# Linear attention followed by a snake MLP on one core: a phased opening, and q transposed by a crossbar DMA from batch 3 on

## The chip, the cores and the metric

The kernel runs on one core of one Trainium2 chip. The metric is the time of one execution on the device in microseconds (us). Of the core's engines the text uses the short names of the profile: PE is TensorE (PEld is its weight load), DVE is VectorE, ACT is ScalarE, POOL is GpSimd, and SP is the engine whose queue issues nearly all DMAs.

## What is computed

The attention is linear: the softmax of q runs over the head's 64 columns, the softmax of k over the sequence, so that k and v collapse to one 64x64 matrix per head. Its output, reshaped to 4608 tokens of 512, goes through two matmuls with a "snake" between them.

```
q, k, v: [8 batches, 8 heads, 576, 64] f32;  w_in [512, 2048], w_out [2048, 512], alpha [2048]
q_s = softmax(q, axis=-1);  k_s = softmax(k, axis=2)
kv  = einsum('bhsd,bhse->bhde', k_s, v)
x   = einsum('bhsd,bhde->bhse', q_s, kv) -> [4608, 512]
h   = x @ w_in
g   = h + sin(alpha*h)**2 / alpha
out = g @ w_out                      # [4608, 512] f32
```

## The kernel before, in words

The schedule is written by hand: every engine runs its instructions in the order in which the program text issues them, and only semaphores and the number of buffers in a pool make one engine wait for another.

**Attention of one batch b.** `exp_q` and `exp_k` (two ACT instructions each, after a load of ACT's Exp table) turn the staged f32 inputs into bf16. `cast_v` copies v. `norm_q` sums q's exponentials on DVE, takes the reciprocal and multiplies (`engs` says on which engine): the result is `qn`, 128 partitions by 2304 bf16. `kv_mm` is 36 small matmuls into `kvp`. `kv_norm` divides on DVE. `q_transpose` makes `qT` out of `qn` by 18 TensorE transposes of 128x128 in two groups (12 and 6) through PSUM, and each group is copied out by `eng`. `attn_out`, called four times, does 4 matmuls each into `xp` and casts the result into `xT`, the transposed input of the MLP. The tiles `kvp`, `tp` (of the transposes) and `xp` share one PSUM slot, the pool `ps_a` with `bufs=1`, so each waits until the one before has been read out. (In the opening, batch 0 has a pool of its own with four.)

**MLP of one tile t of 512 tokens** (9 tiles). The first half, called h(t) here, has 16 slots `ni`. In each, `mm_h` does 4 matmuls of 512 columns into a PSUM tile `hp` (pool `ps_h`, 4 buffers), `sine` applies sin on ACT and squares it on ACT ("A"), POOL ("P") or DVE ("D"), and `combine` on DVE makes the bf16 tile `g`. The second half, o(t), is 64 matmuls `mm_o` for four output blocks j, each copied out by `evac_o` and stored by two DMAs of SP's queue. Exp and Sin need different ACT tables, so each change between them issues an ACT_TABLE_LOAD.

**Stages.** Batch 0's attention comes first, then h(0), o(0) with batch 1's attention at its end, and h(1) with batch 2's attention woven into its slots. From t = 2 on, a stage t holds h(t), o(t-1) and, up to t = 6, the attention of batch b = t+1: after slot 0 the exponentials, casts, `norm_q` on POOL and the loads of the next batch; at slot 4 `kv_mm` and `kv_norm`; at slots 6 and 7 the transposes; at slots 8 to 11 the four `attn_out`. After slot ni, o(t-1) has been advanced to `want` of its 64 matmuls:

```
want = 20 + 11 * ni // 4 if b is not None else 4 * (ni + 1)
```

Inputs and weights pass through a staging pool of 6 buffers (`stage`), so a load is issued only when the buffer six loads earlier has been consumed. All loads and stores stand in one SP queue in program order.

Of the kernel before, what the change touches and what calls it, by code (L numbers as in the profile page):

```python
# [15 lines left out]
F32 = mybir.dt.float32  # L16
BF16 = mybir.dt.bfloat16
# [6 lines left out]
def kernel(  # L24
# [74 lines left out]

    wst = {}  # L100

    def load_win(c):
        st = stage.tile([128, 4, 512], F32, name="st_w", tag="st")
        nc.sync.dma_start(out=st, in_=win_v[:, :, c * 512:(c + 1) * 512])
        wst["i", c] = st

    def load_wout(c):
# [64 lines left out]

# [130 lines left out]
    accs = [ps_o.tile([128, dm], F32, name="op", tag="o") for _ in range(2)]
    accs += [ps_h.tile([128, dm], F32, name="hp", tag="h") for _ in range(2)]
    for ni in range(nN):
        for j in range(4):
            mm_o(0, j, ni, accs[j])
# [3 lines left out]
    cast_v(1, [V, GP])
    for j in range(4):
        evac_o(0, j, accs[j], ACT_CP if j % 2 else DVE_CP)
    load_batch(2)
    for g in range(2):
        q_transpose(1, g, ps_a, ACT_CP)
    kv_mm(1, 0, ps_a)
    kv_mm(1, 1, ps_a)
    kv_norm(1)
    for ii in range(2):  # L320
        attn_out(1, ii, 0, ps_a, DVE_CP)
        attn_out(1, ii, 1, ps_a, ACT_CP)


    def o_stream(t):
        for j in range(4):
            acc = ps_o.tile([128, dm], F32, name="op", tag="o")
            for ni in range(nN):
                mm_o(t, j, ni, acc)
                if ni == nN - 1:  # L330
                    evac_o(t, j, acc, DVE_CP)
                yield

    SQ1 = "PAPDPAPDPAPDPAPA"
    for t in range(1, nT):
        b = t + 1 if t + 1 < B else None
        os = o_stream(t - 1) if t > 1 else None
        done = 0
        pend = None
        for ni in range(nN):  # L340
# [10 lines left out]
            s = sine(t, ni, hp, "A" if t > 1 else SQ1[ni])
            if t == 1:
                if pend:
                    combine(t, *pend)
                pend = (ni, hp, s)
            else:
                combine(t, ni, hp, s)
            if b is not None and ni == 0:
                exp_q(b)
                exp_k(b)  # L360
                cast_v(b, [GP, GP])
                norm_q(b, [GP])
                if b + 1 < B:
                    load_batch(b + 1)
            if os is not None:
                want = 20 + 11 * ni // 4 if b is not None else 4 * (ni + 1)
                while done < min(64, want):
                    next(os)
                    done += 1
        if pend:  # L370
            combine(t, *pend)
        if os is not None:
            for _ in os:
                pass

    for _ in o_stream(nT - 1):
        pass


# [28 lines left out]
```

## Time and profile before

| | before |
|---|---|
| time, median of 3 runs | 339.1 us (338.93 to 339.96) |
| the profiled execution: its time, and the span from first to last instruction | 340.48 us, 338.7 us |
| PE busy | 291.6 us (86%), 1713 matmuls |
| ACT busy | 237.5 us (70%) |
| DVE busy | 200.6 us (59%) |
| POOL busy | 71.7 us (21%) |
| DMA | 46.44 MB, 41.4% of 16 engines |

The span is what the profile divides up; 1.78 us of the profiled execution lie outside it. That execution is 1.4 us longer than the median. PE is the busiest engine, but its 14% of idle time are not spread evenly, and the busy share says nothing about the clock at which the matmuls ran, which the trace gives apart.

### The profile page before, as it was taken

The page shows a single profiled execution, that of the slowest core. Times are in us where ns is not written, and L with a number is a line of the kernel's source. Part 1 is how long each engine was busy: PE and PEld are TensorE (multiplying, and loading weights), DVE is VectorE, ACT ScalarE, POOL GpSimd, SP SyncE. Part 2 cuts the span into 40 slices and gives each one's busy share as a digit, 9 for nine tenths or more (in the row PEclk, how much of TensorE's full clock was granted, in tenths as well). Part 3 has the DMA queues.
Part 4 walks back from the last instruction along what each step waited for, and adds up shares of the span by engine and source line. Part 5 has one row for each costly group of instructions (what it writes and reads, how often), then busy time and mean ns, then how long its engine had stood idle before and what let it go on. Part 6 is the DMA issues. An engine that isn't in the chain of part 4 may idle for free.

```text
span 338.7 us, 4528 instructions
## 1 busy us (share of the span) xinstructions
PE 291.6 (86%) x1713; PEld 134.9 (40%) x1713; DVE 200.6 (59%) x286; ACT 237.5 (70%) x328; POOL 71.7 (21%) x47
## 2 busy tenths in 40 slices
PE   0585895484799899989998999899989999999994
PEld 0432342322334444443444445444534444444441
DVE  3648761206886786487558755874687545555511
ACT  4476862268479867986897789778968777777600
POOL 0456632026443700150024003300400000000000
PEclk9979999556999999999999999999999999999999
DMA  7999903999500111850195029302111111211132
GB/s 266 389 386 387 391 10 76 309 392 391 215 0 0 33 31 33 297 199 19 38 333 173 3 62 362 120 4 59 33 31 31 32 31 33 50 44 33 32 93 62
DMA packets 22758, 46.44 MB, mean 137 GB/s; under 512 B 1728, under 2 KB 1744, under 8 KB 22736
## 3 DMA queue, kind: packets, MB, share of 16 engines
q1 hardware_dynamic: 22736, 46.15, 41.4%
q8 instruction: 13, 0.21, 0.3%
q14 instruction: 9, 0.07, 0.1%
HBM read 36.71 MB, written 9.44 MB: 136 GB/s over the span
## 4 chain that ended last, share of the span: by engine, by line
PE 49%; ACT 21%; DVE 18%; issue 6%; POOL 2%; DMA 2%; SPq 0%; ACTq 0%; POOLq 0%
PE op L229 22%; PE hp L209 20%; ACT s L215 7%; DVE g L225 7%; ACT ke L117 3%; ACT qe L117 3%; ACT L215 2%; ACT L117 2%; ACT s L217 2%; PE xp L196 2%; DVE kvb L168 2%; PE hp L229 2%; DVE s L221 2%; DVE qT L184 2%; PE tp L183 2%
## 5 line engine op out<-in xcount | busy, mean ns | idle before, releaser
L209 PE MATMUL hp<-xT,win 128*128 128x512 bf16 x576 | 150.5, 389 | 12.4 <-DVE g L225 11.4
L225 DVE SCALAR_TENSOR_TENSOR g<-s,inva_sb,hp 128x512 bf16<-128x512 f32 x144 | 105.9, 744 | 70.4 <-ACT s L217 65.2
L229 PE MATMUL op<-wout,g 128*128 128x512 bf16 x544 | 138.6, 380 | 0.0
L215 ACT ACTIVATE s<-hp,alpha_sb 128x512 f32<-128x512 f32 x144 | 97.8, 683 | 49.7 <-PE hp L209 36.8
L209 PEld LDWEIGHTS <-win 128*128 128x128 bf16 x576 | 56.8, 100 | 84.5 <-issue 21.4
L217 ACT ACTIVATE s<-s 128x512 f32<-128x512 f32 x126 | 79.4, 630 | 4.0
L229 PEld LDWEIGHTS <-g 128*128 128x128 bf16 x576 | 53.8, 98 | 63.4 <-issue 0.5
L147 POOL TENSOR_TENSOR qn<-qe,qs 128x2304 bf16<-128x2304 bf16 (+1 forms) x7 | 26.7, 3817 | 115.2 <-PE hp L209 100.7
L145 DVE TENSOR_REDUCE qs<-qe 128x36 f32<-128x2304 bf16 (+1 forms) x10 | 20.7, 2071 | 27.2 <-ACT qe L117 27.2
L234 DVE COPY o<-op 128x512 f32<-128x512 f32 x33 | 22.3, 676 | 14.0 <-PE op L229 14.0
L183 PE MATMUL tp<-identb,qn 128*128 128x128 bf16 x144 | 11.9, 234 | 20.9 <-DVE qn L147 9.2
L199 DVE CAST xT<-xp 128x512 bf16<-128x512 f32 (+1 forms) x28 | 20.8, 745 | 5.5 <-PE xp L196 5.5
L219 POOL TENSOR_TENSOR s<-s 128x512 f32<-128x512 f32 x12 | 12.9, 1076 | 39.4 <-ACT s L215 39.4
L183 PEld LDWEIGHTS <-qn 128*128 128x128 bf16 x144 | 9.8, 104 | 26.7 <-issue 16.3
L117 ACT ACTIVATE qe<-st_q 128x1152 bf16<-128x1152 f32 x16 | 17.8, 1156 | 3.4 <-DMA st_q<-in_q_dram 3.4
L131 POOL CAST vb<-st_v 128x1152 bf16<-128x1152 f32 x14 | 16.9, 1236 | 15.2 <-DMA st_v<-in_v_dram 15.2
L117 ACT ACTIVATE ke<-st_k 128x1152 bf16<-128x1152 f32 x16 | 17.7, 1149 | 0.7 <-DMA st_k<-in_k_dram 0.7
L196 PE MATMUL xp<-qT,kvb 64*64 64x256 bf16 (+1 forms) x128 | 10.4, 320 | 5.4 <-DVE kvb L168 2.5
L156 PE MATMUL kvp<-vb,ke 64*128 64x130 bf16 x288 | 12.4, 252 | 0.9 <-ACT qT L184 0.9
L156 PEld LDWEIGHTS <-ke 64*128 64x128 bf16 x288 | 10.8, 112 | 4.2 <-ACT s L215 3.0
L215 ACT ACT_TABLE_LOAD x8 | 10.3, 1283 | 1.7 <-PE hp L209 1.6
L117 ACT ACT_TABLE_LOAD x8 | 10.3, 1283 | 0.9 <-PEq L392 0.7
(28 smaller groups left out, 75.8 us busy)
## 6 DMA issues: line engine op xcount, KB each, us to landing
out_dram<-o SPq DMA_DIRECT2D x72, 128.0 KB, 2.4
st_q<-in_q_dram SPq DMA_DIRECT2D x7, 1152.0 KB, 6.3
st_k<-in_k_dram SPq DMA_DIRECT2D x7, 1152.0 KB, 9.6
st_v<-in_v_dram SPq DMA_DIRECT2D x7, 1152.0 KB, 11.1
st_w<-in_moe_w_in_dram SPq DMA_DIRECT2D x4, 1024.0 KB, 13.6
st_w<-in_moe_w_out_dram SPq DMA_DIRECT2D x4, 1024.0 KB, 15.7
st_q<-in_q_dram SPq DMA_DIRECT2D x2, 576.0 KB, 4.3
st_k<-in_k_dram SPq DMA_DIRECT2D x2, 576.0 KB, 6.4
```

The lines of the kernel that those rows point to most:

```text
L117: nc.scalar.activation(dst[:, :, ii * 128:(ii + 1) * 128].rearrange("p j (x d) -> p x j d", x=2), src[:, ii::2], AX.Exp)
L145: nc.vector.tensor_reduce(part, src, axis=AXL.X, op=ALU.add)
L147: engs[h].tensor_tensor(dst, src, part.unsqueeze(3).to_broadcast([128, J, w, D]), op=ALU.mult)
L156: nc.tensor.matmul(kvp[:, e, ii * 130:(ii + 1) * 130], ke[r, j, ii * 128:(ii + 1) * 128], vt[r, j, ii * 130:(ii + 1) * 130], start=(j == 0 ...
L183: nc.tensor.transpose(tp[:, h, 2 * jj + ii], qn[:, j, ii * 128:(ii + 1) * 128], identb)
L199: eng(xT[:, ii::2, c0:c0 + n], xp[:, :, 0:n])
L209: nc.tensor.matmul(hp, win[:, ki, ni * 128:(ni + 1) * 128], xT[:, ki, t * MF:(t + 1) * MF], start=(ki == 0), stop=(ki == 3))
L215: nc.scalar.activation(s, hp, AX.Sin, scale=alpha_sb[:, ni:ni + 1])
L217: nc.scalar.activation(s, s, AX.Square)
L225: nc.vector.scalar_tensor_tensor(G[t][:, ni], in0=s, scalar=inva_sb[:, ni:ni + 1], in1=hp, op0=ALU.mult, op1=ALU.add)
L229: nc.tensor.matmul(acc, G[t][:, ni, j * 128:(j + 1) * 128], wout[:, ni, :], start=(ni == 0), stop=(ni == nN - 1))
L234: eng(o, acc)
```

## The change

The stages are taken apart and put in another order up to t = 2, and from batch 3 on `qn` is transposed by one DMA per batch through the DMA engines' crossbar.

- **Opening.** 14 matmuls on a tile that nobody reads (`warm`) stand on PE ahead of batch 0's transposes. The first half of `norm_q(0)` is multiplied on POOL, `cast_v(0)` is all on DVE, a one-element Sin issues the Sin table load ahead of the `xT` casts, and w_in's first chunk is loaded and cast in two parts. All of batches 1 and 2 are loaded ahead of the first stores.
- **h(0)** has 6 PSUM tiles (two of them of `ps_o`, `wide`) and 4 buffers for s, and squares in another rotation. **o(0)** is done in two pairs of blocks; batch 1's attention is woven into the second. **h(1)** stands alone. **o(1)** comes next with batch 2's attention woven in (50 of its 64 matmuls; the other 14 stand behind slot 2 of h(2)). **h(2)** carries batch 3's attention, and half its squares go to POOL.
- **Stages t = 3 to 6** keep their order, but `kv_mm` moves from slot 4 to 5, the transposes of slots 6 and 7 become one DMA_TRANSPOSE of SP's queue issued at slot 7, and the `attn_out` move from slots 8 to 11 to slots 10 to 13. h(7), h(8) and o(8) are as before; the last block is copied by DVE and ACT in halves and stored from two queues.
- `kv_norm` takes one reciprocal in place of two.

```diff
-    spool = ctx.enter_context(tc.tile_pool(name="spool", bufs=3))
+    spool = ctx.enter_context(tc.tile_pool(name="spool", bufs=4))
...
-        kvr = small.tile([128, 2, 2], F32, name="kvr")
+        kvr = small.tile([128, 2, 2, 2], F32, name="kvr")
...
-    def mm_h(t, ni):
+    def mm_h(t, ni, wide=False):
...
-        hp = ps_h.tile([128, MF], F32, name="hp", tag="h")
+        if wide and ni % 6 >= 4:
+            hp = ps_o.tile([128, MF], F32, name="op", tag="o")
+        else:
+            hp = ps_h.tile([128, MF], F32, name="hp", tag="h")
...
+        if last:
+            nc.vector.tensor_copy(o[:, 0:dm // 2], acc[:, 0:dm // 2])
+            nc.scalar.copy(o[:, dm // 2:], acc[:, dm // 2:])
...
+    load("q", q, 1)
+    load("k", k, 1)
+    load("v", v, 1, halves=True)
+    load_batch(2)
...
-        norm_q(0, [V, V])
-        cast_v(0, [GP, V])
...
+        warm = ps_s.tile([128, 4, 128], F32, name="warm", tag="a")
+        for n in range(14):
+            nc.tensor.matmul(warm, identb, A["qe", 0][:, 0:4, 0:128], start=True, stop=True)
+        norm_q(0, [GP, V])
+        cast_v(0, [V, V])
...
+        nc.scalar.activation(zero, zero, AX.Sin)
...
-    SQ0 = "APADAPADAPADAPAA"
...
+    SQ0 = "ADPADPADPADPADPA"
     for ni in range(nN):
...
+        h_slot(0, ni, SQ0[ni], lag, wide=True)
+        flush(lag, 1)
+        if ni in (0, 2, 5):
+            cast_win((0, 2, 5).index(ni) + 1, POOL_CP)
+        elif ni in (8, 11, 14):
+            cast_wout((8, 11, 14).index(ni), POOL_CP)
...
+    exp_q(1)
+    norm_q(1, [GP, V])
+    os = o_pair(0, 0, ps_o)
+    take(os)
+    exp_k(1)
+    cast_v(1, [GP, V])
+    os = o_pair(0, 2, ps_h)
+    take(os, 16)
+    q_transpose(1, 0, ps_a, ACT_CP)
+    take(os, 2)
+    q_transpose(1, 1, ps_a, ACT_CP)
...
+    SQ1 = "PAPDPAPAPPDPAPAP"
+    for ni in range(nN):
+        h_slot(1, ni, SQ1[ni], lag, wide=True)
+        flush(lag, 1)
...
+    attn_front(2, [V, GP])
+    os = o_stream(1)
+    take(os, 32)
+    kv_mm(2, 0, ps_a)
...
+    def attn_back(b, n):
+        if n == 0:
+            kv_mm(b, 0, ps_a)
+            kv_mm(b, 1, ps_a)
+            kv_norm(b)
+        elif n == 2:
+            A["qT", b] = att2.tile([128, J, 2, 128], BF16, name="qT")
+            nc.sync.dma_start(out=A["qT", b].rearrange("p j ii c -> p (j ii) c"),
+                              in_=A["qn", b].rearrange("p j c -> p (j c)"), transpose=True)
+        elif 5 <= n < 9:
+            attn_out(b, (n - 5) // 2, (n - 5) % 2, ps_a, DVE_CP)
+
+    SQ2 = "PAPAPAPAPAPAPAPA"
+    for ni in range(nN):
+        hp = h_slot(2, ni, SQ2[ni], lag)
+        flush(lag, 1)
+        if ni == 2:
+            flush(lag, 0)
+            attn_front(3, [GP])
+            take(os)
+        attn_back(3, ni - 7)
...
             if b is not None:
-                if ni == 4:
-                    kv_mm(b, 0, ps_a)
-                    kv_mm(b, 1, ps_a)
-                    kv_norm(b)
-                elif ni in (6, 7):
-                    q_transpose(b, ni - 6, ps_a, DVE_CP)
-                elif 8 <= ni < 12:
-                    attn_out(b, (ni - 8) // 2, ni % 2, ps_a, DVE_CP)
...
+                attn_back(b, ni - 5)
+            s = sine(t, ni, hp, "A")
+            combine(t, ni, hp, s)
```

How the change moves instructions is shown at three places. The first is SP's queue in one middle stage. Of the kernel before: the loads of the next batch, then the stores of o(t-1), two for each of the four blocks.

```order
L92 DMA st_q<-in_q_dram 128x4x576
L92 DMA st_k<-in_k_dram 128x4x576
L92 DMA st_v<-in_v_dram 128x4x576
L237 DMA out_dram<-o 64x512 x8
L92 DMA st_q<-in_q_dram 128x4x576
```

Of the changed kernel, the same stage:

```order
L92 DMA st_q<-in_q_dram 128x4x576
L92 DMA st_k<-in_k_dram 128x4x576
L92 DMA st_v<-in_v_dram 128x4x576
L248 DMA out_dram<-o 64x512 x4
L420 DMA_TRANSPOSE qT<-qn 128x18x128
L248 DMA out_dram<-o 64x512 x4
```

The transposing DMA stands behind the stores of blocks 0 and 1 and ahead of those of blocks 2 and 3.

The second place is DVE's queue in the same stage, from the copy of block 0 (`o<-op`) to the casts into `xT`. Of the kernel before:

```order
L234 COPY o<-op 128x512
L225 SCALAR_TENSOR_TENSOR g<-s,inva_sb,hp 128x512 x3
L167 RECIPROCAL kvr<-kvp 64x4
L168 TENSOR_TENSOR kvb<-kvp,kvr 64x256
L167 RECIPROCAL kvr<-kvp 64x4
L168 TENSOR_TENSOR kvb<-kvp,kvr 64x256
L225 SCALAR_TENSOR_TENSOR g<-s,inva_sb,hp 128x512 x2
L234 COPY o<-op 128x512
L184 COPY qT<-tp 128x1536
L225 SCALAR_TENSOR_TENSOR g<-s,inva_sb,hp 128x512
L184 COPY qT<-tp 128x768
```

Of the changed kernel:

```order
L244 COPY o<-op 128x512
L231 SCALAR_TENSOR_TENSOR g<-s,inva_sb,hp 128x512 x4
L167 RECIPROCAL kvr<-kvp 128x8
L170 TENSOR_TENSOR kvb<-kvp,kvr 64x256 x2
L231 SCALAR_TENSOR_TENSOR g<-s,inva_sb,hp 128x512
L244 COPY o<-op 128x512
L231 SCALAR_TENSOR_TENSOR g<-s,inva_sb,hp 128x512 x4
L201 CAST xT<-xp 128x2x256
L231 SCALAR_TENSOR_TENSOR g<-s,inva_sb,hp 128x512
L201 CAST xT<-xp 128x2x320
```

The two copies into `qT` are gone, the normalisation of kv stands one combine later, and block 1's copy still stands behind the combine of slot 5.

The third place is ACT's queue between h(0) and h(1). Of the kernel before, where L117 are the exponentials of batch 1 and, at the end, of batch 2:

```order
L117 ACT_TABLE_LOAD
L117 ACTIVATE qe<-st_q 128x2x9x64 x2
L117 ACTIVATE ke<-st_k 128x2x9x64 x2
L234 COPY o<-op 128x512
L234 COPY o<-hp 128x512
L184 COPY qT<-tp 128x1536
L184 COPY qT<-tp 128x768
L199 CAST xT<-xp 128x2x320 x2
L215 ACT_TABLE_LOAD
L215 ACTIVATE s<-hp,alpha_sb 128x512
L117 ACT_TABLE_LOAD
```

Of the changed kernel:

```order
L119 ACT_TABLE_LOAD
L119 ACTIVATE qe<-st_q 128x2x9x64 x2
L244 COPY o<-op 128x512
L119 ACTIVATE ke<-st_k 128x2x9x64 x2
L186 COPY qT<-tp 128x1536
L186 COPY qT<-tp 128x768
L201 CAST xT<-xp 128x2x320 x2
L244 COPY o<-hp 128x512
L221 ACT_TABLE_LOAD
L221 ACTIVATE s<-hp,alpha_sb 128x512 x2
L223 ACTIVATE s<-s 128x512
```

The copies of o(0)'s blocks no longer stand together ahead of the `qT` copies, and the sines of h(1) run on without a change back to the Exp table after slot 0.

## Rows read from the trace of the kernel before

**Rows 1.** Windows: busy us (instructions) per engine; then PE clock, DMA share, GB/s.

```profile
19.57:43.22 23.65, 18.43 (x74) 7.62 (x74) 15.90 (x19) 17.90 (x27) 14.35 (x11) 0.93 1.02 377
43.22:70.24 27.02, 17.61 (x125) 9.06 (x124) 9.00 (x14) 9.54 (x11) 4.68 (x3) 0.77 0.50 158
70.24:100.20 29.96, 22.30 (x133) 9.91 (x133) 20.08 (x29) 20.23 (x26) 13.90 (x10) 0.81 0.67 249
...
133.48:166.28 32.80, 31.59 (x199) 14.53 (x198) 22.36 (x32) 27.34 (x39) 6.32 (x3) 1.00 0.43 141
...
263.50:291.20 27.70, 27.70 (x130) 12.51 (x129) 14.33 (x20) 21.00 (x32) 0.00 (x0) 1.00 0.17 38
```

**Rows 2.** Windows, one stretch of 2 us after PE went idle at 75.9.

```profile
78.00:80.00 2.00, 0.00 (x0) 0.00 (x0) 1.97 (x2) 1.98 (x3) 0.00 (x0) 0.55 1.05 389
```

**Rows 3.** Timeline, batch 0: start, us, what; in brackets the idle time before.

```profile
10.88 1.36 DVE L147 TENSOR_TENSOR qn<-qe,qs 128x1152 bf16<-128x1152 bf16 x1
...
14.22 2.13 PE L156 MATMUL kvp<-vb,ke 64*128 64x130 bf16 x36
...
19.57 6.81 PE L209 MATMUL hp<-xT,win 128*128 128x512 bf16 x23 [0.22 <-ACT xT L199]
```

**Rows 4.** Timeline, h(0): a DVE square beside POOL's casts.

```profile
23.95 3.73 POOL L254 CAST win<-st_w 128x2048 bf16<-128x2048 f32 x2
...
25.79 2.43 DVE L221 TENSOR_TENSOR s<-s 128x512 f32<-128x512 f32 x1 [1.00 <-ACT s L215]
```

**Rows 5.** Groups of instructions by line and shape: busy us, mean ns of one.

```profile
L225 DVE SCALAR_TENSOR_TENSOR g<-s,inva_sb,hp 128x512 bf16<-128x512 f32 x144 | 105.9, 744 | 70.4 <-ACT s L217 65.2 <-POOL s L219 4.9
...
L215 ACT ACTIVATE s<-hp,alpha_sb 128x512 f32<-128x512 f32 x144 | 97.8, 683 | 49.7 <-PE hp L209 36.8 <-DVE g L225 8.8 <-DVE kvr L167 3.0
L217 ACT ACTIVATE s<-s 128x512 f32<-128x512 f32 x126 | 79.4, 630 | 4.0
...
L117 ACT ACTIVATE qe<-st_q 128x1152 bf16<-128x1152 f32 x16 | 17.8, 1156 | 3.4 <-DMA st_q<-in_q_dram 3.4
...
L219 POOL TENSOR_TENSOR s<-s 128x512 f32<-128x512 f32 x12 | 12.9, 1076 | 39.4 <-ACT s L215 39.4
...
L117 ACT ACT_TABLE_LOAD x8 | 10.3, 1283 | 0.9 <-PEq L392 0.7
```

**Rows 6.** Timeline, between h(0) and h(1), and the start of h(1).

```profile
58.06 0.58 ACT L234 COPY o<-hp 128x512 f32<-128x512 f32 x1 [3.00 <-DMA out_dram<-o]
...
60.04 0.80 PE L183 MATMUL tp<-identb,qn 128*128 128x128 bf16 x6 [4.50 <-ACT qT L184]
...
70.24 5.63 PE L209 MATMUL hp<-xT,win 128*128 128x512 bf16 x15 [0.25 <-ACT xT L199]
```

**Rows 7.** Timeline, the stage t = 4, which begins at 166.28.

```profile
166.28 1.03 PE L209 MATMUL hp<-xT,win 128*128 128x512 bf16 x4
...
167.95 1.11 SPq L237 DMA_DIRECT2D out_dram<-o  x2
...
176.74 1.20 PE L156 MATMUL kvp<-vb,ke 64*128 64x130 bf16 x36
...
180.61 0.67 ACT L215 ACTIVATE s<-hp,alpha_sb 128x512 f32<-128x512 f32 x1
...
181.59 0.83 PE L183 MATMUL tp<-identb,qn 128*128 128x128 bf16 x12 [0.74 <-DVE kvb L168]
...
182.79 0.68 DVE L234 COPY o<-op 128x512 f32<-128x512 f32 x1
...
184.39 0.50 PE L183 MATMUL tp<-identb,qn 128*128 128x128 bf16 x6 [0.47 <-DVE qT L184]
```

**Rows 8.** DMA issues: KB each, median us from issue to landing.

```profile
st_q<-in_q_dram SPq DMA_DIRECT2D x2, 576.0 KB, 4.3
...
alpha_rows<-in_moe_alpha_dram SPq DMA_DIRECT2D x1, 8.0 KB, 1.6
```

**Rows 9.** Timeline, the last block's copy.

```profile
333.97 0.69 DVE L234 COPY o<-op 128x512 f32<-128x512 f32 x1 [2.76 <-PE op L229]
```

More of the change, by code (lines that the diff above doesn't have):

```diff
@@ L100, with load_win @@
     wst = {}
-    def load_win(c):
+    def load_win(c, parts=1):
         st = stage.tile([128, 4, 512], F32, name="st_w", tag="st")
-        nc.sync.dma_start(out=st, in_=win_v[:, :, c * 512:(c + 1) * 512])
+        n = 4 // parts
+        for h in range(parts):
+            nc.sync.dma_start(out=st[:, h * n:(h + 1) * n], in_=win_v[:, h * n:(h + 1) * n, c * 512:(c + 1) * 512])
         wst["i", c] = st
@@ L301, with h_slot, flush @@
-    cast_wout(3, POOL_CP)
[L303 to L307, printed above, removed]
+    def h_slot(t, ni, sq, lag, wide=False):
+        hp = mm_h(t, ni, wide)
+        s = sine(t, ni, hp, sq)
+        lag.append((t, ni, hp, s))
+        return lag
+    def flush(lag, keep):
+        while len(lag) > keep:
+            combine(*lag.pop(0))
@@ L308, with take @@
+    def take(it, n=None):
+        for _ in iter(int, 1) if n is None else range(n):
+            if next(it, 0) == 0:
+                return
     exp_q(1)
-    norm_q(1, [V, GP])
+    norm_q(1, [GP, V])
+    os = o_pair(0, 0, ps_o)
+    take(os)
     exp_k(1)
[L311 to L316, printed above, removed]
+    cast_v(1, [GP, V])
+    os = o_pair(0, 2, ps_h)
@@ L317 @@
+    take(os, 16)
+    q_transpose(1, 0, ps_a, ACT_CP)
+    take(os, 2)
+    q_transpose(1, 1, ps_a, ACT_CP)
+    take(os, 2)
     kv_mm(1, 0, ps_a)
@@ L330, in o_stream, with attn_front @@
                 if ni == nN - 1:
-                    evac_o(t, j, acc, DVE_CP)
+                    evac_o(t, j, acc, DVE_CP, last=(t == nT - 1 and j == 3))
                 yield
-    SQ1 = "PAPDPAPDPAPDPAPA"
-    for t in range(1, nT):
+    def attn_front(b, engs):
+        exp_q(b)
+        exp_k(b)
+        cast_v(b, [GP, GP])
+        norm_q(b, engs)
+        if b + 1 < B:
+            load_batch(b + 1)
+    attn_front(2, [V, GP])
+    os = o_stream(1)
+    take(os, 32)
+    kv_mm(2, 0, ps_a)
+    kv_mm(2, 1, ps_a)
+    kv_norm(2)
+    take(os, 4)
+    q_transpose(2, 0, ps_a, DVE_CP)
+    take(os, 3)
+    q_transpose(2, 1, ps_a, DVE_CP)
+    take(os, 3)
+    for n in range(4):
+        attn_out(2, n // 2, n % 2, ps_a, (DVE_CP, ACT_CP)[n % 2])
+        take(os, 2)
+    def attn_back(b, n):
+        if n == 0:
+            kv_mm(b, 0, ps_a)
[8 more added lines that the diff above has]
+    SQ2 = "PAPAPAPAPAPAPAPA"
+    for ni in range(nN):
+        hp = h_slot(2, ni, SQ2[ni], lag)
+        flush(lag, 1)
+        if ni == 2:
+            flush(lag, 0)
+            attn_front(3, [GP])
+            take(os)
+        attn_back(3, ni - 7)
+    flush(lag, 0)
+    for t in range(3, nT):
         b = t + 1 if t + 1 < B else None
-        os = o_stream(t - 1) if t > 1 else None
+        os = o_stream(t - 1)
         done = 0
-        pend = None
         for ni in range(nN):
@@ L342 @@
             if b is not None:
-                if ni == 4:
-                    kv_mm(b, 0, ps_a)
-                    kv_mm(b, 1, ps_a)
-                    kv_norm(b)
-                elif ni in (6, 7):
-                    q_transpose(b, ni - 6, ps_a, DVE_CP)
-                elif 8 <= ni < 12:
-                    attn_out(b, (ni - 8) // 2, ni % 2, ps_a, DVE_CP)
[L351 to L357, printed above, removed]
-            if b is not None and ni == 0:
[L359 to L377, printed above, removed]
+                attn_back(b, ni - 5)
+            s = sine(t, ni, hp, "A")
+            combine(t, ni, hp, s)
+            if b is not None and ni == 0:
+                attn_front(b, [GP])
+            want = 20 + 11 * ni // 4 if b is not None else 4 * (ni + 1)
+            take(os, min(64, want) - done)
+            done = min(64, want)
+        take(os)
+    take(o_stream(nT - 1))
 _INS = ['q', 'k', 'v', 'moe_w_in', 'moe_w_out', 'moe_alpha']
```

62 lines of the change are left out of this document (35 added, 27 removed).

## The prediction

> **What bounds the kernel now.** I read the windows by stage first. A middle stage takes 32.8 us, and PE works in 31.6 of them [rows 1]: from t = 2 to t = 6 PE sets the time, and a stage without attention is PE without a gap, 27.7 us for its 128 matmuls, 0.216 each [rows 1]. The opening is different. h(0) takes 23.65 us, the stretch of o(0) with batch 1's attention 27.02, h(1) with batch 2's attention 29.96 [rows 1]. No engine is busy for all of them, and PE's mean clock falls to 0.77 and 0.81. 64 matmuls of half a tile need 13.8 us (64 x 0.216). So some 80 us hold 192 such matmuls (41.5 us) and the PE work of two batches, and this is where time can come from.
>
> Why each is slow: in h(0) a DVE square that has 0.6 us of work took 2.43 us beside POOL's casts [rows 4]. It was issued at 25.79 and ended 0.54 us after they did (27.68): on these operands DVE and POOL take turns. After o(0) PE waits on one thread: ACT's copy of an output block waits 3.00 us for a store to free its buffer, the `qT` copy stands behind it, and the second transposes wait 4.50 us [rows 6]. From these transposes to the first matmuls of h(1), at 60.04 and 70.24, pass 10.2 us with PE mostly idle [rows 6]. Then PE runs out of PSUM tiles at 75.87 (70.24 + 5.63, [rows 6]) while ACT does batch 2's exponentials, and two to four microseconds later its clock is at 0.55 [rows 2], which is a stretch at its lower level, 1.2 GHz.
>
> **The change, part by part.** I follow the changed order stage by stage and put it against the same point of before.
>
> *Batch 0.* `qn` was ready at 12.24 (10.88 + 1.36, [rows 3]). With POOL multiplying the first half beside DVE's second sum I get 11.65: the two multiplications take turns, so 0.6 us is saved, not 1.36. The 36 `kvp` matmuls took 2.13 us here, against 1.20 in a middle stage [rows 3, 7]; after the `warm` matmuls I take the higher clock, which saves 0.9 there and about as much on the transposes. ACT's `qT` copies and the Sin table (1.28, [rows 5]) then hold back part of it. First matmul of h(0): about 17.6 in place of 19.57 [rows 3], 2.0 earlier.
>
> *h(0).* In three slots POOL does a square (1.08, [rows 5]) and a cast (1.87, half of 3.73, [rows 4]), and DVE's own square (0.6) takes its turn with them: 3.55 us, more than ACT's three sines and one square (2.7) or DVE's work (2.8) [rows 5]. 16 slots: 18.9, and 1.5 to fill. It ends at 38.0; before it ended at 43.22 [rows 1].
>
> *o(0) and batch 1.* PE starts o(0) at about 33.5, ahead of the last combines. It has 13.8 us of o(0) and 3.8 of attention (36 `kvp` at 1.20, 18 transposes at 1.33 [rows 7], some 1.3 for `attn_out`). The shared PSUM slot still makes it wait for each copy, about 3.1 us in all, since matmuls of o(0) fill much of these waits. h(1) starts at 54.2; before, at 70.24 [rows 6].
>
> *h(1) alone.* ACT does 16 sines, 5 squares and a table: 10.9 + 3.2 + 1.3 [rows 5], with 2.2 for filling and the last combine 17.6. It ends at 71.8.
>
> *Batch 2 with 50 matmuls of o(1).* ACT is free at 69.9; a table and four exponentials (1.28 + 4.6, [rows 5]) end at 75.8. The chain from there to h(2) is `kv_mm`, `kv_norm`, transposes, four `attn_out`, which took 10.2 us before [rows 6]; I give it 10.8, because POOL's multiplication ends late. h(2) starts at 86.6.
>
> *h(2) and batch 3.* ACT sets it: two tables to Sin, one to Exp, four exponentials, 16 sines and 8 squares, 3.8 + 4.6 + 10.9 + 5.0 = 24.3 [rows 5]. PE idles some 4 us in it, so I add 1.1 for slots at the lower clock. Stage t = 3 begins at 112.0. Before it began at 133.48 [rows 1], with the same work done. **The opening gives 21.5 us.**
>
> *A middle stage (t = 3 to 6, four times).* Gone are 18 transposes (0.83 + 0.50) and PE's waits ahead of them (0.74 + 0.47) [rows 7]: 2.5 us. The two `qT` copies leave DVE, which has room. `kv_mm`, one slot later, no longer covers the wait for a PSUM tile at slot 5: 0.5 us are added. Without more the stage is 32.8 - 2.5 + 0.5 = 30.8.
>
> The DMA's cost is in no row, so I bound it. It moves 128 x 2304 x 2 bytes = 576 KB. Lower end: 576 KB at the rate of the opening's loads (377 GB/s, [rows 1]) is 1.6 us, and the smallest DMA takes 1.6 us to land [rows 8]: 3.2. Upper end: 18 blocks one after another, each at that 1.6: 28.8. The nearest row is a load of just these 576 KB, 4.3 us from issue to landing [rows 8], and I take that.
>
> What it may hide behind, with the stage's start (166.28, [rows 7]) as zero: `kv_mm` began at 10.46. Now 3 more matmuls of o(t-1), the wait and slot 5 come first, so it begins at 12.5 and ends at 13.7; five slots (20 matmuls) and 13 of o(t-1) later, 7.1 us, PE is at `attn_out`: 20.8. The DMA stands in SP's queue behind block 1's stores, these behind block 1's copy, this on DVE behind slot 5's combine, and this behind slot 5's sine, square and `kv_norm`. The sine began at 14.3 [rows 7]. I get 17.0 for the copy (16.5 before, [rows 7]), 0.68 for it and 1.11 for its two stores [rows 7]: the DMA is issued at 18.8, though `qn` has long been ready. It lands at 23.1, and PE, which takes its matmuls in order, waits 2.3 us at the first `attn_out`; h's later slots and o(t-1) stand behind it. The stage is 33.1 us, 0.3 longer than before. In t = 2 the slots are paced by ACT and there are about 7 us of slack; there I charge nothing.
>
> A page speaks against this edit. The Trainium skill (VectorE: DVE Perf Modes, The three transpose paths) gives 1309 ns for a 128x128 block through the crossbar and 390 ns on TensorE; no row here shows the first, and the transposes in a middle stage come to 0.07 us each. By that figure one block after another would be an estimated 23.6 us per batch, and the sum would be about 395 us. Its page Advanced Engine Details and Errata (X-Bar Transpose) says that such DMAs are as fast as ordinary ones; by that the sum stays as it is here.
>
> *The tail.* The last copy (0.69, [rows 9]) is halved and its two stores (1.11, [rows 7]) go out side by side: 0.7 us.
>
> **The sum**, against the profiled execution: 112.0 + 4 x 33.1 = 244.4 at the start of h(7); from there to the end before, 338.7 - 264.7 (166.28 + 3 x 32.8) = 74.0, now 73.3: a span of 317.7. With the 1.78 us outside the span and the 1.4 by which that execution lies above the median, 318.1 us. Shorter by 21, all of it from the opening.
>
> **The rivals.**
> - *The transpose is hidden.* It needs a landing in under 2 us after issue, or an issue some 2.3 us earlier than I place it. For it: the loads of the stage have landed by then, so the queues are empty. Against it: no DMA of this size in the trace is that quick. Stage 30.8, 309 us.
> - *The waits come dearer, or the opening gives half.* Where the DMA takes 6 us, PE waits 4.0, long enough for its clock to fall as at 78 [rows 2]: stages of 35 to 37. Or the stages of the opening, which I laid out with hardly a hole, keep some 10 us of the old waits. 325 to 333 us.
> - *Block after block (slower).* The crossbar takes the 18 blocks in turn at the 1.6 us of the smallest DMA: 28.8 us, of which 2.0 are hidden; the stage is 57.6 and the kernel 416 us (395 by the page's figure). For it: 18 separate blocks. Against it: ordinary DMAs here use all engines at once. It decides against the kernel from 9.6 us per transpose on, where 4 x (9.6 - 4.3) eats the 21.
> - *The opening changes nothing*, because the loads bound it: DMA share is 1.02 in h(0) [rows 1]. But at 377 GB/s batch 1's q lands by about 36.5, when I first use it, so I give this little.
>
> **How the numbers follow.** My forecast has 0.55 (a transpose of 3.2 to 5.5 us: 314 to 323). Hidden: 0.14. Dearer or half: 0.22. Block after block: 0.06. Nothing gained: 0.03. The range from 307 to 330 leaves out the last two and the end of the third. 0.3% (1 us) is about what a measurement can tell from no change. Faster 0.91, same 0.02, slower 0.07.
>
> **What would show it.** Right: h(0) from about 17.6 to 38, h(1) from 54, h(2) from 87, t = 3 at 112; no wait of DVE's squares over 2 us; in a middle stage the transposing DMA issued just after block 1's stores, PE waiting for `qT` about 2.3 us. Wrong: PE at the lower clock in h(0) or between h(1) and h(2); ACT waiting for stores again between o(0) and h(1); a transpose much over 5 us or under 3; middle stages under 32 or over 35 us.

## The result, and the profile after

The kernel takes 329.83 us, the median of 4 runs (327.36 to 331.88), against 339.41 before on the same chip (338.93 to 339.96). The ratio is 0.9714, with a 95% interval from 0.9644 to 0.9784: 9.6 us faster, inside the predicted range, but less than half of the 21 us that were forecast. The profiled execution is the longest of the four, 331.88 us, with a span of 330.0; the forecast for a span was 317.7. The ratios here and below leave out executions over 1.5% longer than the fastest of their kernel: two of the kernel before, and one, of 353.64 us, of the crossbar alone.

First the page of the changed kernel: busy time, and PE's clock in 40 slices.

```profile
PE 290.2 (88%) x1637; PEld 130.0 (39%) x1637; DVE 191.3 (58%) x271; ACT 231.6 (70%) x321; POOL 83.0 (25%) x58
...
PEclk9959999999996999979999999799999999999999
```

Four slices hold stretches at the lower clock, and they lie in h(0), in h(2) and in two of the middle stages. The windows, with the columns of [rows 1], are h(0), o(0) with batch 1, h(1), o(1) with batch 2, h(2) with batch 3, and the stages t = 3 to 6:

```profile
17.72:39.69 21.97, 20.58 (x80) 8.41 (x80) 16.44 (x21) 16.56 (x24) 17.79 (x11) 0.88 1.05 387
39.69:57.57 17.88, 14.94 (x119) 7.23 (x119) 9.74 (x14) 7.70 (x10) 6.31 (x4) 1.00 0.80 296
57.57:74.73 17.16, 17.00 (x78) 7.54 (x77) 12.52 (x18) 16.63 (x25) 10.81 (x10) 1.00 0.72 238
74.73:89.30 14.57, 11.99 (x106) 5.91 (x107) 10.10 (x15) 4.76 (x6) 3.56 (x3) 1.00 0.16 36
89.30:119.24 29.94, 23.25 (x132) 10.21 (x131) 17.74 (x26) 23.68 (x32) 16.06 (x13) 0.89 0.85 275
119.24:154.29 35.05, 31.81 (x180) 13.76 (x179) 20.05 (x28) 27.00 (x38) 6.91 (x4) 0.95 0.19 40
154.29:187.84 33.55, 30.50 (x182) 13.56 (x180) 20.80 (x29) 27.24 (x39) 6.32 (x3) 1.00 0.52 155
187.84:222.71 34.87, 31.88 (x182) 13.90 (x180) 20.80 (x29) 27.25 (x39) 6.32 (x3) 0.95 0.50 150
222.71:256.25 33.54, 30.50 (x181) 13.60 (x180) 20.80 (x29) 27.24 (x39) 4.05 (x1) 1.00 0.24 50
```

Against [rows 1] the account of the 8.7 us of span (338.7 to 330.0) has three lines. The opening ends at 119.24 and not at 133.48: 14.2 won. The four middle stages sum to 137.0 and not to 4 x 32.8 = 131.2: 5.8 lost. From h(7), at 256.25, to the end it is 73.75 and not 74.0: 0.25 won. So the change is two changes of opposite sign, and the middle stages give back some 40% of what the opening wins. That the crossbar DMA is the cause is what the experiments below show.

How a middle stage loses is seen in t = 3. First SP's queue and PE in its timeline (start, length, instruction, idle time before), then the DMA's row among the issues (median us from issue to landing):

```profile
128.53 9.22 SPq L248 DMA_DIRECT2D out_dram<-o  x4
137.87 2.84 SPq L420 DMA_TRANSPOSE qT<-qn  x1
...
138.92 1.03 PE L215 MATMUL hp<-xT,win 128*128 128x512 bf16 x4
142.81 0.43 PE L198 MATMUL xp<-qT,kvb 64*64 64x256 bf16 x4 [2.87 <-DMA qT<-qn]
```

```profile
st_q<-in_q_dram SPq DMA_DIRECT2D x2, 576.0 KB, 4.4
...
qT<-qn SPq DMA_TRANSPOSE x5, 4.7
```

The DMA stands behind block 1's stores and is issued at 137.87, 18.6 us into the stage; it lands 4.7 to 4.9 us later, and PE stands still for 2.87 us. The other three stages show 2.67, 2.62 and 2.67, 10.8 us in all. In t = 2 there is no wait: issued at 104.25, needed at 111.99.

What comes behind the wait differs. Windows of 1 us in t = 3 (us; busy us by engine; clock, DMA share, GB/s):

```profile
140.00:141.00 1.00, 0.00 (x0) 0.00 (x0) 0.75 (x1) 0.97 (x3) 0.00 (x0) 1.00 1.17 216
141.00:142.00 1.00, 0.00 (x0) 0.00 (x0) 0.00 (x0) 0.33 (x1) 0.00 (x0) 1.00 1.11 204
142.00:143.00 1.00, 0.19 (x4) 0.13 (x4) 0.00 (x0) 0.00 (x0) 0.00 (x0) 0.82 0.05 13
143.00:144.00 1.00, 1.00 (x6) 0.28 (x3) 0.71 (x2) 0.00 (x0) 0.00 (x0) 0.50 0.09 16
...
146.00:147.00 1.00, 1.00 (x8) 0.42 (x8) 0.43 (x1) 0.69 (x1) 0.00 (x0) 0.98 0.00 0
```

PE stood still, then its clock was at 0.50 (1.2 GHz) for some 3.5 us of matmuls. In this execution that happened in t = 3 and t = 5 and not in t = 4 and t = 6, though the idle times ahead of it are alike. From the first `attn_out` to the first matmuls of o in the next stage it took 12.3 and 12.2 us in those two (142.81 to 155.15, 211.38 to 223.57) and 10.8 in t = 4 (177.89 to 188.70): 1.4 to 1.5 us for the clock.

### The profile page after: what moved, and what is told of

Its sections match the earlier page's. It is cut to its first block, busy times and chain, and to the rows that moved or that the text cites. A ratio compares the mean times of both kernels' runs of the same rounds, so it can differ in the third digit from the quotient of the medians.

```text
span 330.0 us, 4367 instructions
## 1 busy us (share of the span) xinstructions
PE 290.2 (88%) x1637; PEld 130.0 (39%) x1637; DVE 191.3 (58%) x271; ACT 231.6 (70%) x321; POOL 83.0 (25%) x58
## 4 chain that ended last, share of the span: by engine, by line
PE 33%; ACT 15%; DMA 6%; issue 6%; DVE 3%; SPq 1%
PE op L235 18%; PE hp L215 14%; ACT s L221 6%; DMA qT<-qn 6%; ACT ke L119 3%; DVE g L231 2%; ACT L221 2%; ACT L119 2%; ACT qe L119 1%; PE xp L198 1%; SPq L248 1%; ACT s L223 1%; DVE o L244 1%; DVE xT L201 0%; DVE o L241 0%
## 5 line engine op out<-in xcount | busy, mean ns | idle before, releaser
L215 PE MATMUL hp<-xT,win 128*128 128x512 bf16 x544 | 141.9, 392 | 8.9 <-DVE g L231 6.2
L231 DVE SCALAR_TENSOR_TENSOR g<-s,inva_sb,hp 128x512 bf16<-128x512 f32 x136 | 99.8, 745 | 73.1 <-ACT s L223 57.6
L235 PE MATMUL op<-wout,g 128*128 128x512 bf16 x544 | 136.8, 382 | 1.7 <-DVE o L244 0.8
L221 ACT ACTIVATE s<-hp,alpha_sb 128x512 f32<-128x512 f32 x136 | 92.1, 683 | 49.2 <-PE hp L215 43.8
L223 ACT ACTIVATE s<-s 128x512 f32<-128x512 f32 x115 | 72.4, 630 | 3.7
L225 POOL TENSOR_TENSOR s<-s 128x512 f32<-128x512 f32 x22 | 25.3, 1154 | 38.4 <-ACT s L221 38.3
L147 DVE TENSOR_REDUCE qs<-qe 128x18 f32<-128x1152 bf16 (+1 forms) x11 | 20.8, 1888 | 16.9 <-ACT qe L119 16.9
L244 DVE COPY o<-op 128x512 f32<-128x512 f32 x32 | 21.5, 674 | 7.1 <-PE op L235 7.1
L198 PE MATMUL xp<-qT,kvb 64*64 64x256 bf16 (+1 forms) x128 | 10.2, 312 | 14.8 <-DMA qT<-qn 10.8
L119 ACT ACTIVATE ke<-st_k 128x1152 bf16<-128x1152 f32 x16 | 17.7, 1150 | 1.3 <-DMA st_k<-in_k_dram 1.3
L198 PEld LDWEIGHTS <-kvb 64*64 64x64 bf16 x128 | 4.6, 104 | 27.4 <-issue 12.9
L201 ACT CAST xT<-xp 128x640 bf16<-128x640 f32 x6 | 4.1, 693 | 15.8 <-PE xp L198 15.8
L227 DVE TENSOR_TENSOR s<-s 128x512 f32<-128x512 f32 x7 | 7.8, 1119 | 4.9 <-ACT s L221 4.9
```

What stands on the lines that cost most here:

```text
L119: nc.scalar.activation(dst[:, :, ii * 128:(ii + 1) * 128].rearrange("p j (x d) -> p x j d", x=2), src[:, ii::2], AX.Exp)
L147: nc.vector.tensor_reduce(part, src, axis=AXL.X, op=ALU.add)
L201: eng(xT[:, ii::2, c0:c0 + n], xp[:, :, 0:n])
L215: nc.tensor.matmul(hp, win[:, ki, ni * 128:(ni + 1) * 128], xT[:, ki, t * MF:(t + 1) * MF], start=(ki == 0), stop=(ki == 3))
L221: nc.scalar.activation(s, hp, AX.Sin, scale=alpha_sb[:, ni:ni + 1])
L223: nc.scalar.activation(s, s, AX.Square)
```

## The experiments

All are timed against the kernel before, in the same job.

**The transposing DMA issued early**, at the slot of `kv_mm` (slot 5), ahead of it and of block 1's stores, and not at slot 7:

```diff
         if n == 0:
+            A["qT", b] = att2.tile([128, J, 2, 128], BF16, name="qT")
+            nc.sync.dma_start(out=A["qT", b].rearrange("p j ii c -> p (j ii) c"),
+                              in_=A["qn", b].rearrange("p j c -> p (j c)"), transpose=True)
             kv_mm(b, 0, ps_a)
...
-        elif n == 2:
-            A["qT", b] = att2.tile([128, J, 2, 128], BF16, name="qT")
...
```

> The changed kernel with the transposing DMA issued two slots earlier, at kv_mm's slot and so ahead of block 1's stores in SP's queue. Theory A (the middle stages lose their time because the transpose is issued late, and PE's clock falls in some of these waits): the wait of 2.7 us for qT goes, the clock stays up, a middle stage is 30.8 to 31.2 us in place of 33.6 or 35.0, and the kernel takes 316 to 320 us. Theory B (the transfer is slowed by the loads of the next batch, which are still under way when it is issued): the transpose takes 8 us or more in place of 4.7, PE still waits 2 us or more at attn_out, and the time stays at 326 to 331 us.

Measured: 316.33 us (314.64 to 317.84), ratio 0.934 [0.9294, 0.9387]. Its timeline in t = 3, SP's queue and PE, and the windows of t = 3 and t = 4:

```profile
125.44 1.12 SPq L248 DMA_DIRECT2D out_dram<-o  x2
129.08 2.74 SPq L416 DMA_TRANSPOSE qT<-qn  x1
133.55 15.95 SPq L248 DMA_DIRECT2D out_dram<-o  x6
...
135.83 1.03 PE L215 MATMUL hp<-xT,win 128*128 128x512 bf16 x4
136.78 0.30 PE L198 MATMUL xp<-qT,kvb 64*64 64x256 bf16 x4
```

```profile
116.15:146.73 30.58, 30.00 (x175) 13.45 (x179) 19.99 (x28) 26.99 (x38) 6.89 (x4) 1.00 0.23 49
146.73:177.54 30.81, 30.17 (x178) 13.60 (x180) 20.75 (x29) 27.25 (x39) 6.32 (x3) 1.00 0.59 169
```

The DMA is issued 12.9 us into the stage in place of 18.6. It now takes 4.6 to 5.7 us to land, more than before, and nobody waits for it. The stages take 30.6 to 30.8 us: the 30.8 that the prediction gave for a hidden transpose, 14.0 us less over four stages than in the changed kernel. Theory A holds.

**The transposes of batch 3 and up on TensorE**, everything else as in the changed kernel:

```diff
-        elif n == 2:
-            A["qT", b] = att2.tile([128, J, 2, 128], BF16, name="qT")
...
+        elif n in (2, 3):
+            q_transpose(b, n - 2, ps_a, DVE_CP)
```

> The changed kernel with the crossbar part alone undone: batches 3 to 7 are transposed by TensorE again, in the two slots after kv_mm's next one, all else as changed. Theory A (as it is issued, the crossbar DMA costs more than the 18 transposes): middle stages of 32.8 to 33.2 us with no fall of the clock in them, 325 to 328 us. Theory B (the crossbar part is where the change gained): 332 us or more.

Measured: 324.8 us (322.97 to 325.69), ratio 0.9568 [0.9532, 0.9604], just under theory A's range, as its stages are: t = 3 to 6 take 32.13, 32.35, 32.36 and 32.35 us, at a clock of 1.00. So against TensorE's transposes in the same place the crossbar, as issued here, costs 1.2 us in a stage whose clock stays up (33.55) and 2.5 to 2.9 in one where it falls (34.87, 35.05), and it gains 1.5 when issued early. By the medians it costs 5.0 us.

**The crossbar alone**: the opening of before, with the new order of the attention steps and the transposing DMA from batch 3 on.

```diff
...
-                if ni == 4:
+                if b >= 3:
+                    attn_back(b, ni - 5)
+                elif ni == 4:
                     kv_mm(b, 0, ps_a)
...
```

> The kernel before with the crossbar part alone: batches 3 to 7 transposed by DMA, with kv_mm, the DMA and attn_out at the slots that the changed kernel gives them in a middle stage; the opening as before. Theory A: each of five stages gets 0.8 to 2.2 us longer, 343 to 350 us. Theory B: each gets shorter by up to 2 us, 329 to 338 us.

Measured: 348.72 us (346.44 to 353.64), ratio 1.0258 [1.0201, 1.0314]. The trace is that of the longest execution. What it says of PE's idle time ahead of instructions that read `qT` (us, times):

```profile
  DMA qT<-qn: 14.7, 5
```

That part of the change alone makes the kernel before slower, by 8.7 us as the ratio has it. Theory A holds. In the trace each of the five stages has a wait of 2.8 to 3.2 us, and the lower clock follows in four of them; of t = 3 to 6 the one where it does not takes 33.79 us, the others 35.28 to 36.75.

**The clock held in h(2)**: 18 matmuls that nobody reads behind slot 6, where PE stands still.

```diff
+        if ni == 6:
+            hold = ps_a.tile([128, 512], F32, name="hold", tag="a")
+            for n in range(18):
+                nc.tensor.matmul(hold, identb, wout[:, 0, :], start=True, stop=True)
         attn_back(3, ni - 7)
```

> The changed kernel with 18 matmuls of 512 columns into a tile that nobody reads behind slot 6 of h(2), where PE idled 3.9 us and its clock then fell. Theory A (the lower clock held up h(2): ACT waited 2.5 us for a PSUM tile there): the clock stays at its upper level, t = 3 begins 2 to 3 us earlier and the kernel takes 326.5 to 328 us. Theory B (h(2) is paced by ACT and by DVE's casts whatever PE's clock): within 0.7 us of the changed kernel, 329 to 330.5 us.

Measured: 329.02 us (328.31 to 331.78), ratio 0.9714 [0.9671, 0.9758]: by time theory B, no difference from the changed kernel that the intervals show. The trace says why. The clock stayed at 1.00, the `kvp` matmuls took 1.20 us and not 2.13, and then PE waited 1.30 us for DVE in their place. h(2) took 28.5 us (87.50 to 116.03), 1.4 less than in the changed kernel's profile; but the kernel with the early DMA, whose `kvp` ran at the lower clock, took only 28.7 (87.42 to 116.15). There the clock was low for some 3.5 us (101 to 104.5) and in the changed kernel's profile for some 6.5 (102 to 108.5). With DVE in the way, the clock is worth between 0.2 and 1.4 us of the 4.5 by which h(2) is too long.

**The cast ahead of the combine in h(2)**, on top of the early DMA:

```diff
         hp = h_slot(2, ni, SQ2[ni], lag)
+        attn_back(3, ni - 7)
         flush(lag, 1)
...
-        attn_back(3, ni - 7)
```

> The kernel with the early transposing DMA (316.33 us), and in h(2) the attention step of a slot is issued before the combine of the slot before, so that the cast of xp into xT no longer stands on DVE behind a combine that waits for POOL's square. Theory A (DVE's order makes the last four slots of h(2) 1.8 us each; ACT's pace there is 1.35): they come to about 5.4 us in place of 7.3, PE's waits for xT in h(2) (1.07, 0.22 and 1.29) go under 0.5 us in all, t = 3 starts near 114.5 in place of 116.15, the time is 314.0 to 315.5. Theory B (POOL's squares and ACT set the slots, the casts only lie in their shadow): the waits move from xT to the PSUM tiles of h, t = 3 starts within 0.6 us of 116.15, 315.8 to 316.8.

Measured: 314.63 us (314.14 to 314.67), ratio 0.9262 [0.9236, 0.9288]. h(2) took 27.73 us (88.47 to 116.20) in place of 28.73; PE's waits for `xT` in it fell from 2.58 us to 1.22, not under 0.5. The signs are split. The time lies in theory A's range, but so do the better two of the four executions without this edit (314.64, 314.86; the others 317.8). And t = 3 starts at 116.20, not near 114.5: h(2) itself started 1.05 us later here, behind an h(0) that ran partly at the lower clock (0.75 over its first 6 us). So the gain of 1.0 us, in place of some 1.65, is read from h(2) in one trace of each; the times do not settle it.

**`qn` of batch 3 multiplied on DVE and POOL**, on top of that one:

```diff
-            attn_front(3, [GP])
+            attn_front(3, [V, GP])
```

> As the one before, and batch 3's qn is multiplied half on DVE and half on POOL (before: all on POOL, 4.05 us from 98.30, with the square of slot 4 standing behind it until 102.30 and DVE's combine waiting 2.70 us for that square). Theory A (POOL's multiplication stands ahead of the squares and holds DVE, ACT and the PSUM tiles): the wait of 2.70 goes under 1 us, h(2) is another 1.0 to 1.5 us shorter than in the kernel before it. Theory B (ACT's exponentials and tables set the first slots; DVE's half takes turns with POOL's half and nothing is won): within 0.5 us of the kernel before it.

Measured: 313.7 us (313.44 to 315.29), ratio 0.9246 [0.9218, 0.9273]. DVE's wait for POOL's square fell from 2.70 us to 1.38, not under 1, and h(2) to 27.40, only 0.3 less: theory B for the stage. The median is 0.9 us lower, but the executions of the two kernels overlap (up to 315.29 here, from 314.14 there). Behind that wait stood another, PE at the lower clock, to which the last run but one comes.

**Matmuls that nobody reads ahead of h(0)**, on top of the early DMA: 3 behind `kv_mm(0)` and 5 behind `attn_out(0)`.

```diff
             kv_mm(0, ii, ps_s)
+        for n in range(3):
+            nc.tensor.matmul(warm, identb, A["qe", 0][:, 0:4, 0:128], start=True, stop=True)
         kv_norm(0)
...
+        warm = ps_s.tile([128, 4, 128], F32, name="warm", tag="a")
+        for n in range(5):
+            nc.tensor.matmul(warm, identb, A["qe", 0][:, 0:4, 0:128], start=True, stop=True)
```

> The kernel with the early transposing DMA, and 3 and 5 matmuls that nobody reads on PE between batch 0's kvp and xp and between xp and h(0), where PE stands idle 0.75 and 1.36 us. The runs of that kernel fall into two groups, 314.6 to 314.9 and 317.8 us, and the clock in the first slots of h(0) was 0.50 in some profiles and 1.00 in others. Theory A (PE's gaps there decide whether the clock falls): all runs lie at 314.5 to 315.5. Theory B (the clock in h(0) is not set by these gaps): runs on both sides, 3 us apart, as before; the median may be anywhere from 314.7 to 318.2.

Measured: 315.19 us (314.91 to 315.5), ratio 0.9282 [0.9256, 0.9308]. The first 16 matmuls of h(0) in the changed kernel, and the first 15 here, with ACT's first exponentials of batch 1 as the last line:

```profile
17.72 6.29 PE L215 MATMUL hp<-xT,win 128*128 128x512 bf16 x16 [1.02 <-ACT xT L201]
```

```profile
16.85 1.24 PE L309 MATMUL warm<-qe,identb 128*128 128x512 bf16 x5 [0.41 <-DVE xT L201]
17.93 3.62 PE L215 MATMUL hp<-xT,win 128*128 128x512 bf16 x15
...
38.94 2.22 ACT L119 ACTIVATE qe<-st_q 128x1152 bf16<-128x1152 f32 x2 [2.67 <-DMA st_q<-in_q_dram]
```

All four runs have a granted clock of 0.995 and lie within 0.6 us, where the kernel without these matmuls has two runs at 314.6 and 314.9 (0.994) and two at 317.8 (0.978). The last run but one below has the same edit, and its five runs agree too. Theory A: PE's idle time ahead of h(0) is what lets the clock fall in some executions. From the first matmul of h(0) to the second half of o(0)'s first two blocks it takes 22.1 us in the changed kernel (17.72 to 39.84) and 19.7 here (17.93 to 37.62), so the lower clock costs 2.4 up to there. At the start of h(1) only 1.5 of it are left (57.57 against 56.03): with the clock up, ACT waits 2.67 us for batch 1's q to land, at 38.9, the last line above. The prediction's rival that the loads bound the opening, which reckoned with 36.5, is true of this stretch. The matmuls themselves cost about 0.4 us against the better group.

**Matmuls that nobody reads in the wait for `qT`**, in the changed kernel:

```diff
         elif 5 <= n < 9:
+            if n == 5 and b > 3:
+                hold = ps_a.tile([128, 512], F32, name="hold", tag="a")
+                for _ in range(12):
+                    nc.tensor.matmul(hold, identb, wout[:, 0, :], start=True, stop=True)
             attn_out(b, (n - 5) // 2, (n - 5) % 2, ps_a, DVE_CP)
```

> The changed kernel as given (329.83 us, its four middle stages 35.1, 33.6, 34.9 and 33.7 us), with 12 matmuls that nobody reads (12 x 0.216 = 2.6 us) on PE ahead of the first attn_out of the stages t = 3 to 6, where PE waits 2.6 to 2.9 us for the transposing DMA. Theory A (of a long stage's cost against 30.8, some 2.7 us are the wait itself and 1.3 are matmuls at the lower clock after PE has stood still): PE is busy through the wait, the clock stays at 1.00, all four stages take 33.4 to 33.8 us, the kernel 326 to 328.5 us. Theory B (the longer stages have another cause): two of them stay near 35 us, 329 to 331 us.

Measured: 328.64 us (327.18 to 330.38), ratio 0.9678 [0.9644, 0.9711]: 1.2 us less than the changed kernel, which its runs' spread doesn't settle. The trace does. The clock was at 1.00 in all four stages, and from the first `attn_out` to the first matmuls of the next o it took 10.82, 10.81 and 10.82 us in t = 3 to 5, against 12.3, 10.8 and 12.2. But the stages were not all 33.4 to 33.8. In t = 3 and t = 5, which took 34.16 and 34.28, the DMA held SP's queue 3.2 and 3.5 us, landed up to 5.5 us after issue, and PE waited another 0.92 and 0.82 us behind the 12 matmuls. So the price of the lower clock is shown; that it is all that sets the long stages apart is not.

**All of it together**: early DMA, cast first, shared multiplication, the matmuls ahead of h(0), and 17 more behind slot 6 of h(2).

> The early transposing DMA, the cast before the combine and the shared multiplication in h(2) (313.7 us), with the matmuls that nobody reads ahead of h(0) (3 and 5) and 17 more behind slot 6 of h(2), where PE stands idle 3.9 us and its clock falls. Theory A (with DVE and POOL out of the way, what holds h(2) back is PE at the lower clock: ACT waits 1.72 us for a PSUM tile behind 4 matmuls of 1.61 and a kvp of 2.13 us): these come to 1.0 and 1.2 us, ACT's wait goes under 0.8, t = 3 starts 1.0 to 1.5 us earlier against the start of h(2), all runs lie at 311.8 to 313.0. Theory B (the clock in h(2) costs nothing, as in the changed kernel with such matmuls alone): 313.0 to 314.0.

Measured: 312.17 us (312.1 to 312.76), ratio 0.9201 [0.918, 0.9222]. PE in h(2):

```profile
96.72 3.83 PE L435 MATMUL hold<-wout,identb 128*128 128x512 bf16 x16
100.78 1.02 PE L215 MATMUL hp<-xT,win 128*128 128x512 bf16 x4 [0.22 <-DVE g L231]
101.73 1.20 PE L158 MATMUL kvp<-vb,ke 64*128 64x130 bf16 x36
...
113.68 0.59 PE L215 MATMUL hp<-xT,win 128*128 128x512 bf16 x2 [0.74 <-DVE xT L201]
```

h(2) takes 26.2 us (87.46 to 113.68), 1.2 less than without the 17 matmuls, and the runs lie within 0.7 us. Theory A: with DVE and POOL out of the way, the clock in h(2) is worth 1.2 us. This version beats both kernels, the one before by 27.0 us and the changed one, timed in another job, by 17.7 us.

**The DMA in ACT's queue**, at the same place in the program of the changed kernel:

```diff
-            nc.sync.dma_start(out=A["qT", b].rearrange("p j ii c -> p (j ii) c"),
+            nc.scalar.dma_start(out=A["qT", b].rearrange("p j ii c -> p (j ii) c"),
```

> The changed kernel as given (329.83 us), with the transposing DMA at the same place in the program but in ACT's queue and not SP's. Theory A (it is late because it stands behind block 1's stores in SP's queue): it is issued 1 to 2.5 us earlier against the stage's start than the 18.6 of SP's queue, PE waits 0.3 to 1.7 us for qT in place of 2.6 to 2.9, the clock stays up, stages of 31 to 32.5 us, 319 to 325 us. Theory B (the issue itself, which held SP's queue for 2.8 us, holds ACT as long, and the sines behind it come late): ACT stands still about 2.8 us per stage; the DMA is earlier, but the PSUM tiles of h run out, and the stages stay at 33 to 35 us, 326 to 331 us.

Measured: 328.06 us (327.73 to 329.33), ratio 0.9669 [0.9644, 0.9695]. Its timeline: ACT in t = 3, PE there, and PE in h(2):

```profile
138.96 2.74 ACTq L420 DMA_TRANSPOSE qT<-qn  x1
141.80 0.69 ACT L221 ACTIVATE s<-hp,alpha_sb 128x512 f32<-128x512 f32 x1 [2.27 <-DVE g L231]
...
144.38 0.30 PE L198 MATMUL xp<-qT,kvb 64*64 64x256 bf16 x4 [0.83 <-DMA qT<-qn]
```

```profile
114.95 0.43 PE L198 MATMUL xp<-qT,kvb 64*64 64x256 bf16 x4 [3.79 <-DMA qT<-qn]
```

Both theories were half right. The DMA is issued 16.1 us into the stage (138.96, the stage having begun at 122.84), 2.5 earlier than in SP's queue; PE waits 0.8 us, and t = 3 and t = 4 take 32.3 and 32.5 us, as theory A has it. The issue holds ACT's queue 2.5 to 2.7 us in a middle stage, and ACT stands still 2.1 to 2.3 us, as theory B has it, but its slack there covers that. In h(2), which ACT sets, nothing covers it: there the DMA comes at 109.1 and holds ACT's queue 3.8 us, PE waits 3.79 us, h(2) takes 34.4 us (29.9 in the changed kernel's profile), and t = 3 begins 3.6 us later. The time is in theory B's range.

## Why the prediction was off

By its own steps, span against span (317.7 forecast, 330.0 measured, 12.3 apart). Two steps failed by most: h(2) with batch 3, 4.5 us too long, and the four middle stages, 4.6 in all.

- **Batch 0** was right: the first matmul of h(0) came at 17.72, forecast 17.6; the `kvp` matmuls ran at the higher clock, 0.69 for each half.
- **h(0)** ended at 39.69 and not at 38.0. "PE at the lower clock in h(0)" was on the list of what would show the forecast wrong. It is what happened, and the run with matmuls ahead of h(0) shows that filling PE's idle time there removes it. With the clock up, as in that run, the same point is at 37.6; three slots take 3.28 us there, by the starts of POOL's casts (25.84, 29.12, 32.40), forecast 3.55.
- **o(0) and batch 1** took 17.88 us, forecast 16.2 (38.0 to 54.2). The term for waits, 3.1 us, was laid out without POOL's last cast of w_out, which holds PE 0.64 us. This I read from the trace alone; no run tested it, and the other 1.0 us stays open.
- **h(1) alone** (17.16, forecast 17.6) and **batch 2 with o(1)** (14.57, forecast 14.8) were right.
- **h(2) and batch 3** is the step that failed by most: 29.94, forecast 25.4. The sum of ACT's work was right (23.68 busy, forecast 24.3). The allowance of 1.1 us for all else was not: ACT stood idle 6.3 us. DVE runs its instructions in program order, so the casts into `xT` stood behind combines that waited for POOL's squares, and these behind POOL's multiplication of `qn`. This is the changed kernel's DVE and PE:

```profile
105.26 2.06 DVE L231 SCALAR_TENSOR_TENSOR g<-s,inva_sb,hp 128x512 bf16<-128x512 f32 x3 [2.70 <-POOL s L225]
...
117.71 0.75 DVE L231 SCALAR_TENSOR_TENSOR g<-s,inva_sb,hp 128x512 bf16<-128x512 f32 x1 [0.59 <-POOL s L225]
118.37 0.82 DVE L201 CAST xT<-xp 128x640 bf16<-128x640 f32 x1
```

```profile
102.61 1.86 PE L215 MATMUL hp<-xT,win 128*128 128x512 bf16 x4 [3.89 <-DVE g L231]
104.40 2.13 PE L158 MATMUL kvp<-vb,ke 64*128 64x130 bf16 x36
...
119.24 0.81 PE L215 MATMUL hp<-xT,win 128*128 128x512 bf16 x3 [1.42 <-DVE xT L201]
```

  The cast of 0.82 us at 118.37 is the one that PE waits 1.42 us for, and ahead of it stands the combine that had waited 0.59 for POOL. Taking these out one by one, on top of the early DMA (28.73), brought h(2) to 27.73, 27.40 and, with the clock held, 26.2. Of the 4.5 us that is 2.5; another 1.2 is the longer stretch at the lower clock in this profile than in that of the early DMA, a reading of two traces; 0.8 stays open.
- **A middle stage** is the second: 33.55 and 33.54 in two stages, 35.05 and 34.87 in the others, forecast 33.1. The chain was right, and the landing a little too cheap: issue at 18.6 (forecast 18.8), 4.7 to 4.9 us to land (4.3), and PE waited 2.6 to 2.9 us (2.3). That is 0.5 of it. The other 1.4, in half the stages, is the lower clock behind the wait, which I had put into a rival for waits of 4.0 us; it came at 2.6 to 2.9. That part of "the waits come dearer" came true, and it, h(2) and h(0) together are most of the 12.3 us.
- **The opening gives 21.5** became 14.2, by h(0), o(0) with batch 1, and h(2).
- **"All of it from the opening"**, with the crossbar about even, was wrong. Alone it costs 8.7 us, and against TensorE's transposes in the new order it costs about 5 as issued. The rival of the hidden transpose had its condition right ("an issue some 2.3 us earlier"): an issue 5.7 us earlier gave the stage of 30.8, but it takes an edit.
- **Block after block** did not happen: 18 blocks in 4.7 us, 0.26 us each. The 1309 ns that the Trainium skill gives for a 128x128 block (VectorE: DVE Perf Modes, The three transpose paths), taken once per block, is not what the trace shows for one DMA over 18 blocks; here the measurement decides. The Trainium skill's other sentence, that such DMAs are as fast as ordinary ones (Advanced Engine Details and Errata, X-Bar Transpose), agrees by the time to landing, 4.7 us against 4.4 for a load of the same 576 KB. By rate it does not: 204 to 216 GB/s while the DMA ran, against 387 in h(0)'s loads.
- **The tail** gave 0.25 of the 0.7.

## What to carry to other kernels

An off-engine transpose is worth what its place in the queue makes it: look for what it stands behind (here two stores, themselves behind a DVE copy) and issue it as soon as its input is ready, since against TensorE's transposes the same DMA lost 1.2 to 2.9 us per stage at one place and won 1.5 at another. Where a stage is laid out by the busiest engine's sum, check the in-order neighbours too: a cast behind a combine behind another engine's square cost about as much as the sum's whole allowance of 1.1 us. And where PE idles for one to four microseconds, as in this case, price the matmuls behind it at both clock levels, because it took the lower one in some executions and stages and not in others.

## What was not expected of the hardware

- The issue of a transposing DMA of 576 KB held its queue 2.5 to 4.1 us, whether SP's or ACT's; the stores of 128 KB hold SP's about 0.55 each (two in 1.11, [rows 7]).
- While it ran, the 16 DMA engines were full (share 1.11 to 1.17) at 204 to 216 GB/s; loads at a share of 1.05 move 387.
- PE's idle times of 2.87, 2.67, 2.62 and 2.67 us, in stages that are otherwise alike, were followed by the lower clock in the first and third and not in the others. The length alone does not tell them apart: with the clock held in h(2) it followed a wait of 2.60 us, and with the crossbar alone it did not follow one of 2.91. Likewise h(0) began at the lower clock behind 1.02 us of idle time in the changed kernel, and at the upper one behind 1.36 in the kernel with the early DMA. What tells them apart stays open.
